# Blocks 0 and 1 of an attention and two-layer MLP kernel: the low part of a weight moves ahead on VectorE, PSUM banks turn otherwise, squares get four pairs of buffers, and a ring has four slots

## The chip, the cores and the metric

The kernel runs on one core of one Trainium2 chip. The metric is the device time of one launch in microseconds (us). Three runs of the kernel before took 1746.13, 1746.9 and 1747.65 us; the median is 1746.9 us.

## The reference

Keys and values are averaged over groups of eight positions, attention runs on those, and two matrix products with an activation between them follow, twice:

```python
scores = scale * np.matmul(q, k_p.transpose(0, 1, 3, 2))      # (8, 8, 576, 72)
attn = softmax(scores)
x = (attn @ v_p) as rows                                      # (4608, 512)
h = np.maximum(x @ w_in, 0.0);  x = h * h @ w_out             # first layer, 512 -> 2048 -> 512
h = x @ w_in2;                  out = np.maximum(0.01 * h, h) @ w_out2
```

## The kernel before, in words

The 4608 token rows are cut into nine blocks of 512. All numbers of a matrix product stand as a high and a low part, and a product is three matmuls: high by high, high by low, low by high. The hidden width of 2048 is cut into 16 chunks of 128.

Blocks 0 and 1 are done together, ahead of the others, because the weights arrive as 64-bit words while they run. `first_products` goes through 32 units, one for each pair of block and chunk, in the order of `ORDER`: chunks 0 to 11 of block 0, chunks 0 to 3 of block 1, chunks 12 to 15 of block 0, chunks 4 to 15 of block 1. A unit is 12 matmuls at L866 into one PSUM bank out of three (`acc_bank`, L863), a ReLU on ScalarE (L876) that empties the bank into a buffer `r`, and a store of `r` to the scratch tensor `mid` in DRAM, issued by GpSimd (L1056). From unit 20 on the buffers are a ring of eight slots, two tiles `xh` and `xl` (L1050). In units 1 to 11 the attention of block 1 runs beside the products (`second_attention`): maxima (L599), exponentials (L608), normalizing (L619 to L629), transposes on TensorE, their high copies on ScalarE (L660) and low parts on VectorE (L669), and the value products L701 to L704 with their split L678/L679.

The weights are converted meanwhile. One weight tile holds two chunks and passes through five steps, "a" to "e": a is ScalarE (L231); b is VectorE's L235 and L238; c is L249 and L252; d is VectorE's L293 and then ScalarE's copy L296, the high part; e is VectorE's L300, the low part, which reads what L296 wrote. `conversion(u)` starts tile n at the units of the table `begins`: every second unit for the first tiles (tile 5 begins at unit 8, tile 6 at 10, tile 7 at 12), and then at units 14, 16, 19, 21, 24, 26 and 29 for tiles 8 to 14. The beginning unit issues a of tile n+1 and c, d of tile n; the unit behind it issues b of tile n+1 and then e of tile n.

`second_products` then takes the 32 units again in order of block and chunk. It loads `r` from `mid` (L1066, on SP's queue), squares it on ScalarE (L879), splits the square into `gh` and `gl` on VectorE (L884, L885, two buffers each) and adds 12 matmuls (L905) to four accumulators, the banks 0 to 3. Beside it go the steps of block 2's attention, one now and then, and the conversion of the second layer's weights. The load runs six units ahead (`AHEAD`), the square three; in the last unit of `first_products` three squares are issued ahead of that unit's ReLU (L1041). Later blocks (`block`) and the second layer follow.

Every engine takes its instructions in the order in which the program issues them; no scheduler changes it.

Of the kernel before, what the change touches and what calls it, by code (L numbers as in the profile page):

```python
# [9 lines left out]
F32 = mybir.dt.float32  # L10
F32R = mybir.dt.float32r
# [5 lines left out]
P = 128  # L17
# [26 lines left out]
def attention_relu2_leaky_kernel(  # L44
# [21 lines left out]
    KC = DM // P  # L66
    FC = DFF // P
    RD = POOL * D
    RROWS = 6 * REM
    T = 512  # L70
# [27 lines left out]
    def sb(shape, dt, tag):  # L98
        pool = POOLS.get(tag, attn)
        return pool.tile(shape, dt, tag=tag, name=tag, bufs=BUFS.get(tag, 1))  # L100

    def bank():
        return psum.tile([P, 512], F32, tag="ps", name="ps", bufs=4)

    def acc_bank(m):
        return psum.tile([P, 512], F32, tag=f"acc{m}", name=f"acc{m}")

    def f32(ap):
        return ap.bitcast(F32)
# [209 lines left out]
    class Stored:  # L319
# [46 lines left out]
        def finish(self):  # L366
            while self.n < 12 * FC:
                self.tick()
# [312 lines left out]
    def x_tiles(dt=F32R):  # L681
        both = [sb([P, KC, T], dt, tag) for tag in ("xh", "xl")]
        return tuple([t[:, kc] for kc in range(KC)] for t in both)
# [166 lines left out]
    def value_steps(blk, t0):  # L850
        def piece(b):
            if b not in built:
                built.add(b)
                v_place(b)
            o, e = max(t0, b * S) - t0, min(t0 + T, (b + 1) * S) - t0
            values(blk, o, e - o)

        return [lambda b=b: piece(b) for b in batches_of(t0)]


    def first(blk, c, at=None):
        hi, lo = xsplit[blk]
        ps = bank() if at is None else acc_bank(at % (KC - 1))  # L863
        for kc in range(KC):
            for n, (w, x) in enumerate(((wih[c], hi), (wih[c], lo), (wil[c], hi))):
                nc.tensor.matmul(  # L866
                    ps,
                    lhsT=w[:, kc],
                    rhs=x[kc],
                    start=(kc == 0 and n == 0),  # L870
                    stop=(kc == KC - 1 and n == 2),
                )
        return ps

    def relu(r, ps):
        nc.scalar.activation(out=r, in_=ps, func=AF.Relu)  # L876

    def square(r):
        nc.scalar.activation(out=r, in_=r, func=AF.Square)  # L879

    def in_parts(r):
        gh = sb([P, T], F32R, "gh")
        gl = sb([P, T], F32R, "gl")
        nc.vector.tensor_copy(gh, r)  # L884
        nc.vector.tensor_tensor(out=gl, in0=r, in1=f32(gh), op=ALU.subtract)  # L885
        return gh, gl

    def between(blk, ps):
        r = sb([P, T], F32, "r")
        relu(r, ps)  # L890
        square(r)
        return in_parts(r)

    def second(c, acc, g):
        gh, gl = g
        wh, wl = woh[c], wol[c]
        ms = range(KC)
        passes = (wh, gh), (wl, gh), (wh, gl)
        if c < FC - 1:
            order = [(m, n) for m in ms for n in (0, 1)] + [(m, 2) for m in ms]  # L900
        else:
            order = [(m, n) for m in ms for n in (0, 1, 2)]
        for m, n in order:
            w, x = passes[n]
            nc.tensor.matmul(  # L905
                acc[m],
                lhsT=w[:, m * P : (m + 1) * P],
                rhs=x,
                start=(c == 0 and n == 0),
                stop=(c == FC - 1 and n == 2),  # L910
            )
# [14 lines left out]
    def block(blk, t0, steps, turn, chunk_done):  # L926
# [4 lines left out]
        def slot(i):  # L931
            nonlocal done
            upto = len(steps) if i >= N_SLOTS - 1 else len(steps) * (i + 1) // N_SLOTS
            while done < upto:
                steps[done]()
                done += 1

        g = between(blk, first(blk, 0))
        chunk_done("in", 0)
        for u in range(FC):  # L940
# [17 lines left out]
    w1, w2 = Weights(w1_in, w1_out), Stored(w2_in, w2_out)  # L958
# [13 lines left out]
    def second_attention():  # L972


        pe, behind, dve = ([[] for _ in range(FC)] for _ in range(3))
        blk, b = 1, 1
        pe[0] += [pooled_late[0], lambda: k_mask(b)]
        behind[0].append(lambda: k_transpose(b) or [])

        def both(u, fn):  # L980
            pe[u].append(lambda: dve[u].extend(fn()))

        for j, i in enumerate(range(T // P, 2 * T // P)):
            u = 1 + 2 * j
            pe[u].append(lambda i=i: (q_transpose(i), taken(("q", i))))
            both(u + 1, lambda i=i: score_products(i))
            dve[u + 2].append(lambda i=i: normalize(i))
            behind[u + 3].append(lambda i=i: [p_products(i, blk, T)])
        for n, (what, c) in enumerate([("v", c) for c in range(NP)] + [("rem", c) for c in range(2)]):
            both(3 + n, lambda what=what, c=c: [v_tile_pe(b, what, c)])  # L990
        turn = value_steps(blk, T)
        pe[6].append(turn[0])
        dve[9].append(lambda: v_split(b))

        def placed():
            built.add(b)
            v_place(b)

        pe[10].append(placed)
        pe[HEAD - 1].append(turn[1])  # L1000
        return pe, behind, dve

    def loads_of(u):

        if u < 2:
            load_q(6 + u)
        if u == 0:
            for c in range(NP):
                load_to(("v", 1, c), v_load(1, c), ("st", "st", "st", "gh")[c])
            for c in range(2):  # L1010
                load_to(("rem", 1, c), rem_load(1, c), "gl")
        if u == 0:
            w1.load(4)
        if u % 2 and u // 2 + 5 < FC - 1:
            w1.load(u // 2 + 5)
        if u == 2 * FC - 12:
            held.clear()
            load()


    begins = {2 * n - 2 if n < FC // 2 else FC - 2 + (n - FC // 2) * 5 // 2: n for n in range(1, FC - 1)}

    def conversion(u):
        if u in begins:
            n = begins[u]
            if n + 1 < FC - 1:
                w1.do("a", n + 1)
            w1.do("bcd" if n == 1 else "cd", n)
        elif u - 1 in begins:
            n = begins[u - 1]  # L1030
            if n + 1 < FC - 1:
                w1.do("b", n + 1)
            w1.do("e", n)

    def first_products():
        pe, behind, dve = second_attention()
        for u, (blk, c) in enumerate(ORDER):
            for fn in pe[u] if u < FC else ():
                fn()
            if u == 2 * FC - 1:  # L1040
                for n in range(3):  # L1041
                    square(mids[n])
                mids["parts"] = in_parts(mids.pop(0))
            ps = first(blk, c, u)
            rest = [x for fn in (behind[u] if u < FC else ()) for x in fn()]
            for fn in dve[u] if u < FC else ():
                fn()
            conversion(u)
            if u == FC + SIDE:
                ring.extend(x for t in x_tiles(F32) for x in t)  # L1050
            r = ring[c % len(ring)] if u >= FC + SIDE else sb([P, T], F32, "r")
            relu(r, ps)
            for fn in rest:
                fn()
            loads_of(u)
            nc.gpsimd.dma_start(out=mid[blk, c], in_=r)  # L1056
            if u >= 2 * FC - AHEAD:
                mid_load(u - 2 * FC + AHEAD)


    ring, mids, AHEAD = [], {}, 6

    def mid_load(u):
        if u < 2 * FC:
            r = mids[u] = ring[u % len(ring)]
            nc.sync.dma_start(out=r, in_=mid[u // FC, u % FC])  # L1066

    def second_products():
        steps, turn = all_steps[2], value_steps(2, 2 * T)
        n_units, done = 2 * FC, 0  # L1070
        w1.load(FC - 1)
        g = mids.pop("parts")
        for u in range(n_units):
            blk, c = divmod(u, FC)
            if c == 0:
                acc = [acc_bank(m) for m in range(KC)]
            mid_load(u + AHEAD)
            if u + 3 < n_units:
                square(mids[u + 3])
            if u + 1 < n_units:  # L1080
                g_next = in_parts(mids.pop(u + 1))
            if u >= n_units - 2:
                turn.pop(0)()
            second(c, acc, g)
            if 4 <= u < 9:
                w1.do("abcde"[u - 4], FC - 1)
            upto = len(steps) * u // (n_units - 3)
            while done < min(upto, len(steps)):
                steps[done]()
                done += 1  # L1090
            if u >= FC // 2:
                w2.tick()
            if c == FC - 1:
                finish(blk * T, acc)
            g = g_next
# [364 lines left out]
```

## Time and profile before

| What | Value |
|---|---|
| Median of three runs | 1746.9 us |
| The profiled execution's own time | 1745.2 us |
| Its span in the trace | 1743.3 us |
| TensorE (PE) busy | 1696.8 us, 97% of the span |
| VectorE (DVE) busy | 1110.9 us, 64% |
| ScalarE (ACT) busy | 627.8 us, 36% |
| First products of blocks 0 and 1 | 47 to 171.5 us |
| Second products of blocks 0 and 1 | 171.5 to 280 us |

The shares are means over the whole span. The change touches the first 280 us only, where TensorE is not always busy; times of the rows below are microseconds from the start of the span, the second number is a duration, and a bracket says how long the engine stood idle before the instruction and what ended that.

### The profile page before, as it was taken

To read this page: it belongs to the slowest core of one execution; us is meant where nothing else is said; L and a number is where in the kernel's file an instruction comes from. 1 tells how busy PE (TensorE), PEld (TensorE's weight loads), DVE (VectorE), ACT (ScalarE), POOL (GpSimd) and SP (SyncE) were. 2 spreads that over 40 slices of the span, in tenths; PEclk is the share of its full clock that TensorE was granted. 3 is DMA by queue.
4 is the path that set the end of the run, shared out by engine and by line. 5 is a ranking of instruction groups with operands and counts; after the bars stand their busy time and mean duration, and the time that the engine had idled before them with its cause. 6 is when DMAs were issued, how large, how long until landed. Compare 5 with 4: busy or idle time off the path is not lost.

```text
span 1743.3 us, 21699 instructions
## 1 busy us (share of the span) xinstructions
PE 1696.8 (97%) x8312; PEld 1462.6 (84%) x8312; DVE 1110.9 (64%) x2020; ACT 627.8 (36%) x1496; POOL 19.1 (1%) x39
## 2 busy tenths in 40 slices
PE   6889999999999999999999999999999999999999
PEld 5768778888888888888888899999899999999998
DVE  7888777666666666565434655665566675666564
ACT  4555244343443443433433322332332332233221
POOL 0012000000000000000000000000000000000000
PEclk9989999999999999999999999999999999999999
DMA  8914552323233332231004202202202411320320
GB/s 231 340 64 141 176 184 87 100 81 95 87 97 86 102 103 67 96 117 61 13 24 151 83 8 73 73 0 73 73 18 104 169 38 72 109 93 17 109 73 37
DMA packets 106296, 162.44 MB, mean 93 GB/s; under 512 B 44112, under 2 KB 44240, under 8 KB 105168
## 3 DMA queue, kind: packets, MB, share of 16 engines
q1 hardware_dynamic: 103632, 152.67, 26.4%
q0 software_dynamic: 2560, 8.39, 1.3%
q8 instruction: 65, 1.06, 0.3%
q14 instruction: 39, 0.32, 0.1%
HBM read 111.75 MB, written 49.28 MB: 92 GB/s over the span
## 4 chain that ended last, share of the span: by engine, by line
PE 90%; DVE 7%; ACT 2%; issue 1%; DMA 0%; SPq 0%; DVEq 0%; ACTq 0%
PE acc L905 20%; PE ps L1281 20%; PE ps L866 17%; PE acc L1348 15%; PE ps L1348 7%; PE acc L866 4%; PE ps L587 2%; PE ps L650 1%; PE ps L551 1%; ACT s L608 1%; PE ps L702 0%; PE ps L704 0%; PE ps L701 0%; PE ps L703 0%; DVE xl L679 0%
## 5 line engine op out<-in xcount | busy, mean ns | idle before, releaser
L905 PE MATMUL acc<-gh,wo 128*128 128x512 f32 x1152 | 297.6, 396 | 4.0 <-DVE gh L884 1.9
L866 PE MATMUL ps<-xh,wi 128*128 128x512 f32 x896 | 297.0, 394 | 0.0
L1281 PE MATMUL ps<-fh,wi 128*128 128x384 f32 x1344 | 289.1, 337 | 0.1
L1281 PEld LDWEIGHTS ps<-fh,wi 128*128 128x128 f32 x1344 | 243.1, 188 | 22.2 <-DVE gh L1294 0.4
L905 PEld LDWEIGHTS acc<-gh,wo 128*128 128x128 f32 x1152 | 213.9, 189 | 50.9 <-DVE gh L884 4.0
L1348 PE MATMUL acc<-wo,sh 128*128 128x512 f32 x768 | 205.6, 390 | 0.0
L866 PEld LDWEIGHTS ps<-xh,wi 128*128 128x128 f32 x896 | 168.2, 188 | 34.9 <-issue 0.2
L884 DVE CAST gh<-r 128x512 fp32r<-128x512 f32 x112 | 47.7, 426 | 199.4 <-ACT r L879 199.0
L866 PE MATMUL ps<-xl,wi 128*128 128x512 f32 x448 | 174.5, 390 | 0.0
L1281 PE MATMUL ps<-fl,wi 128*128 128x384 f32 x672 | 171.1, 336 | 0.0
L905 PE MATMUL acc<-gl,wo 128*128 128x512 f32 x576 | 159.7, 391 | 0.0
L1348 PEld LDWEIGHTS acc<-wo,sh 128*128 128x128 f32 x768 | 141.5, 188 | 15.6
L876 ACT ACTIVATE r<-ps 128x512 f32<-128x512 f32 x112 | 67.7, 604 | 212.0 <-PE ps L866 212.0
L905 PEld LDWEIGHTS acc<-gl,wo 128*128 128x128 f32 x576 | 108.8, 189 | 23.5
L1281 PEld LDWEIGHTS ps<-fl,wi 128*128 128x128 f32 x672 | 121.4, 188 | 0.0
L1348 PE MATMUL acc<-wo,sl 128*128 128x512 f32 x384 | 120.3, 392 | 0.0
L608 ACT ACTIVATE s<-ps,m 128x72 f32<-128x72 f32 x240 | 72.3, 331 | 102.0 <-DVE m L599 102.0
L1348 PE MATMUL ps<-wo,sh 128*128 128x512 f32 x384 | 102.8, 389 | 0.0
L1294 DVE TENSOR_TENSOR u<-gh,ps 128x384 f32<-128x384 f32 x48 | 26.6, 554 | 119.0 <-PE ps L1281 119.0
L866 PEld LDWEIGHTS ps<-xl,wi 128*128 128x128 f32 x448 | 84.2, 188 | 16.6
L1348 PEld LDWEIGHTS acc<-wo,sl 128*128 128x128 f32 x384 | 72.1, 188 | 18.3 <-DVE sl L1329 3.7
L885 DVE TENSOR_TENSOR gl<-r,gh 128x512 fp32r<-128x512 f32 x112 | 77.6, 693 | 7.7 <-PE acc L905 0.5
(206 smaller groups left out, 2366.4 us busy)
## 6 DMA issues: line engine op xcount, KB each, us to landing
wi<-in_moe_w_in SPq DMA_DIRECT2D x8, 1024.0 KB
wo<-in_moe_w_out SPq DMA_DIRECT2D x8, 1024.0 KB
val<-in_moe_w_in SPq DMA_DIRECT2D x16, 512.0 KB
val<-in_moe_w_out SPq DMA_DIRECT2D x16, 512.0 KB
w2p<-val SPq DMA_DIRECT2D x16, 512.0 KB
wo<-w2p SPq DMA_DIRECT2D x8, 1024.0 KB
xh<-x SPq DMA_DIRECT2D x10, 768.0 KB
xl<-x SPq DMA_DIRECT2D x10, 768.0 KB
```

The costliest lines, as they stand in the source:

```text
L551: nc.tensor.transpose(ps[:, cc * P : (cc + 1) * P], raw[:, cc * P : (cc + 1) * P], ident)
L587: nc.tensor.matmul(ps[: r0 + n, c2 * PAIR : (c2 + 1) * PAIR], lhsT=qt[:, cc, : r0 + n], rhs=kts[b][:, keys], start=True, stop=True,)
L608: nc.scalar.activation(out=s[:, g, :], in_=ps[:, h * SP : (h + 1) * SP], func=AF.Exp, bias=m[:, g : g + 1], accum_out=None if i in early e ...
L650: nc.tensor.transpose(ps[:, cc * P : (cc + 1) * P], flat[:, cc * PAIR : cc * PAIR + P], ident)
L866: nc.tensor.matmul(ps, lhsT=w[:, kc], rhs=x[kc], start=(kc == 0 and n == 0), stop=(kc == KC - 1 and n == 2),)
L876: nc.scalar.activation(out=r, in_=ps, func=AF.Relu)
L884: nc.vector.tensor_copy(gh, r)
L885: nc.vector.tensor_tensor(out=gl, in0=r, in1=f32(gh), op=ALU.subtract)
L905: nc.tensor.matmul(acc[m], lhsT=w[:, m * P : (m + 1) * P], rhs=x, start=(c == 0 and n == 0), stop=(c == FC - 1 and n == 2),)
L1281: nc.tensor.matmul(at, lhsT=w[:, FORMS[j], kc], rhs=x[j][:, kc], start=m == 0 and j in (0, 1, 4), stop=m == 5, skip_group_check=True,)
L1294: nc.vector.tensor_tensor(out=out_, in0=x, in1=at, op=ALU.add)
L1348: nc.tensor.matmul(self.acc[i], lhsT=x[g % 2][c][t][:, at], rhs=self.outs[p][:, part_, c], start=p == 0 and m == 0, stop=p == PAIRS - 1 an ...
```

## The change

Five things move, all in blocks 0 and 1.

- Step e of a tile leaves `conversion` and is issued earlier in its unit: ahead of the attention's VectorE work of that unit (`dve[u]`) and ahead of step b of the next tile.
- `first` takes bank (u + 2) mod 3 in place of u mod 3.
- The ring has four slots, the tile `xh`; the tile `xl` becomes two further pairs of buffers for the squares' parts (`more`), taken in turn with the old ones.
- `AHEAD` is 4 in place of 6, the square runs two units ahead in place of three, and two squares in place of three stand ahead of the last ReLU.
- In units 15 and 31 of `second_products` no step of block 2's attention is issued.

```diff
     def first(blk, c, at=None):
         hi, lo = xsplit[blk]
-        ps = bank() if at is None else acc_bank(at % (KC - 1))
+        ps = bank() if at is None else acc_bank((at + 2) % (KC - 1))
...
-    def in_parts(r):
-        gh = sb([P, T], F32R, "gh")
-        gl = sb([P, T], F32R, "gl")
+    def in_parts(r, to=None):
+        gh, gl = to or [sb([P, T], F32R, tag) for tag in ("gh", "gl")]
...
                 w1.do("b", n + 1)
-            w1.do("e", n)
...
             if u == 2 * FC - 1:
-                for n in range(3):
+                for n in range(2):
                     square(mids[n])
                 mids["parts"] = in_parts(mids.pop(0))
             ps = first(blk, c, u)
             rest = [x for fn in (behind[u] if u < FC else ()) for x in fn()]
+            if u - 1 in begins:
+                w1.do("e", begins[u - 1])
             for fn in dve[u] if u < FC else ():
                 fn()
             conversion(u)
             if u == FC + SIDE:
-                ring.extend(x for t in x_tiles(F32) for x in t)
+                one, two = sb([P, KC, T], F32, "xh"), sb([P, KC, T], F32R, "xl")
+                ring.extend(one[:, n] for n in range(KC))
+                more.extend((two[:, n], two[:, n + 1]) for n in (0, 2))
...
-    ring, mids, AHEAD = [], {}, 6
+    ring, more, mids, AHEAD = [], [], {}, 4
...
-            if u + 3 < n_units:
-                square(mids[u + 3])
+            if u + 2 < n_units:
+                square(mids[u + 2])
             if u + 1 < n_units:
-                g_next = in_parts(mids.pop(u + 1))
+                g_next = in_parts(mids.pop(u + 1), more[(u + 1) % 2] if (u + 1) % 4 > 1 and u + 3 < n_units else None)
...
-            while done < min(upto, len(steps)):
+            while c < FC - 1 and done < min(upto, len(steps)):
```

On VectorE in unit 9 of the first products, between the low parts of a transposed tile (L669) and the normalizing of the next (L619), the rows stand like this; `wi_907` is the tile whose low part unit 10 multiplies by:

```order
 L669 TENSOR_TENSOR ptl<-ps,pth 128x4x128
 L669 TENSOR_TENSOR ptr<-ps,ptr 32x2x128
+L300 TENSOR_TENSOR wi_907<-val,wi_907 128x1024
 L619 TENSOR_REDUCE l<-s 128x8
 L620 TENSOR_SCALAR l<-l 128x8
```

Before, that L300 stood behind the whole normalizing, the split of the values and L235, L238 of the next tile; now it stands ahead of them. Units 3, 5 and 7 show the same move.

On VectorE from unit 12 on, where only weights are left, each tile has this piece (`wo_1101` is one tile, `wo_947` the words of the next):

```order
 L293 TENSOR_TENSOR val<-val,wo_852 128x1024
+L300 TENSOR_TENSOR wo_1101<-val,wo_1101 128x1024
 L235 TENSOR_SCALAR val<-wo_947 128x1024
 L238 SCALAR_TENSOR_TENSOR val<-wo_947,val 128x1024
-L300 TENSOR_TENSOR wo_1101<-val,wo_1101 128x1024
 L249 TENSOR_SCALAR wo_947<-val 128x1024
 L252 SCALAR_TENSOR_TENSOR wo_947<-wo_947 128x1024
 L293 TENSOR_TENSOR val<-val,wo_947 128x1024
```

L235 and L238 stood between L293 and the L300 that waits for ScalarE's copy of its result; now L300 follows L293 at once.

On ScalarE at the end of the first products, before (the three L876 are the ReLUs of units 29, 30 and 31):

```order
L296 CAST wo_1408<-val 128x1024
L876 ACTIVATE xl<-acc_1392 128x512
L876 ACTIVATE xl<-acc_1413 128x512
L879 ACTIVATE xh<-xh 128x512 x3
L876 ACTIVATE xl<-acc_1437 128x512
```

And now, in the same place:

```order
L296 CAST wo_1406<-val 128x1024
L876 ACTIVATE xh<-acc_1390 128x512
L876 ACTIVATE xh<-acc_1411 128x512
L879 ACTIVATE xh<-xh 128x512 x2
L876 ACTIVATE xh<-acc_1434 128x512
```

The second of the two squares reads ring slot 1, which now holds unit 29's result until that is stored and chunk 1 of block 0 is loaded into it; before, chunks 0 to 2 were loaded in units 26 to 28, into slots that units 24 to 26 had used.

## Rows read from the trace of the kernel before

**Rows 1.** The page's busy line: busy us (share) xinstructions of each engine.
```profile
PE 1696.8 (97%) x8312; PEld 1462.6 (84%) x8312; DVE 1110.9 (64%) x2020; ACT 627.8 (36%) x1496; POOL 19.1 (1%) x39
```

**Rows 2.** Two stretches: us, busy of PE, PEld, DVE, ACT, POOL, granted clock, DMA.
```profile
100.00:110.00 10.00, 5.80 (x16) 4.42 (x16) 7.06 (x10) 2.15 (x7) 0.69 (x2) 0.50 0.15 54
130.00:140.00 10.00, 10.00 (x46) 8.28 (x45) 9.83 (x10) 4.80 (x7) 2.71 (x5) 1.00 0.35 130
```

**Rows 3.** Timeline of PE, first products: start, us, instruction, idle before and its releaser.
```profile
46.82 0.47 PE L866 MATMUL acc<-xh,wi 128*128 128x512 f32 x1 [2.09 <-DVE qt L391]
...
54.90 1.39 PE L587 MATMUL acc<-kt,qt 128*128 128x144 f32 x8 [1.08 <-ACT qt L556]
...
98.75 0.50 PE L866 MATMUL acc<-xh,wi 128*128 128x512 f32 x1 [1.60 <-ACT wi L296]
...
104.20 1.22 PE L866 MATMUL acc<-xh,wi 128*128 128x512 f32 x2 [4.71 <-DVE wi L300]
```

**Rows 4.** Timeline of DVE in units 5 to 10.
```profile
72.43 0.75 DVE L619 TENSOR_REDUCE l<-s 128x8 f32<-128x576 f32 x1 [0.55 <-ACT s L608]
...
85.39 0.75 DVE L619 TENSOR_REDUCE l<-s 128x8 f32<-128x576 f32 x1 [0.28 <-ACT s L608]
...
96.80 0.75 DVE L619 TENSOR_REDUCE l<-s 128x8 f32<-128x576 f32 x1 [0.55 <-ACT s L608]
...
101.07 0.68 DVE L235 TENSOR_SCALAR val<-wi 128x1024 uint32<-128x1024 uint32 x1
...
110.34 0.69 DVE L669 TENSOR_TENSOR ptl<-ps,pth 128x512 fp32r<-128x512 f32 x1 [3.07 <-ACT pth L660]
```

**Rows 5.** Timeline of ACT in units 5 and 7.
```profile
73.28 1.07 ACT L296 CAST wi<-val 128x1024 fp32r<-128x1024 f32 x1
...
86.23 1.08 ACT L296 CAST wi<-val 128x1024 fp32r<-128x1024 f32 x1
```

**Rows 6.** Timeline of DVE, weights alone: one round, and the last tile.
```profile
126.79 1.23 DVE L293 TENSOR_TENSOR val<-val,wo 128x1024 f32<-128x1024 f32 x1
127.93 0.69 DVE L235 TENSOR_SCALAR val<-wo 128x1024 uint32<-128x1024 uint32 x1
128.65 1.23 DVE L238 SCALAR_TENSOR_TENSOR val<-wo,val 128x1024 uint32<-128x1024 uint32 x1
129.79 1.22 DVE L300 TENSOR_TENSOR wo<-val,wo 128x1024 fp32r<-128x1024 f32 x1
...
131.66 1.23 DVE L252 SCALAR_TENSOR_TENSOR wo<-wo 128x1024 f32<-128x1024 uint32 x1
132.93 1.23 DVE L293 TENSOR_TENSOR val<-val,wo 128x1024 f32<-128x1024 f32 x1
...
163.59 1.23 DVE L293 TENSOR_TENSOR val<-val,wo 128x1024 f32<-128x1024 f32 x1
165.93 1.23 DVE L300 TENSOR_TENSOR wo<-val,wo 128x1024 fp32r<-128x1024 f32 x1 [1.11 <-ACT wo L296]
```

**Rows 7.** Timeline of ACT at the end of the first products.
```profile
164.85 1.05 ACT L296 CAST wo<-val 128x1024 fp32r<-128x1024 f32 x1 [0.69 <-DVE val L293]
...
169.50 1.66 ACT L879 ACTIVATE xh<-xh 128x512 f32<-128x512 f32 x3
171.72 0.60 ACT L876 ACTIVATE xl<-acc 128x512 f32<-128x512 f32 x1 [0.56 <-ACT xh L879]
```

**Rows 8.** Stores of L1056 from issue to landing.
```profile
DMA to landing us min/median/max: 2.3/2.6/8.5
```

**Rows 9.** Timeline of SP: the load of `mid` for unit 7.
```profile
181.28 0.32 SPq L1066 DMA_DIRECT2D xl<-mid  x1
```

**Rows 10.** Timeline of ACT: the square that waited for that load.
```profile
184.11 0.63 ACT L879 ACTIVATE xl<-xl 128x512 f32<-128x512 f32 x1 [1.85 <-DMA xl<-mid]
```

**Rows 11.** Timeline of PE: the start of the second products.
```profile
172.37 1.67 PE L905 MATMUL acc<-gh,wo 128*128 128x512 f32 x6 [0.28 <-ACT xl L876]
```

**Rows 12.** The page's groups: L905, busy, mean ns, idle before and its largest releaser.
```profile
L905 PE MATMUL acc<-gh,wo 128*128 128x512 f32 x1152 | 297.6, 396 | 4.0 <-DVE gh L884 1.9
```

## The prediction, made before the run

> **What bounds the kernel now.** I read the busy line first: TensorE works 97% of the span [rows 1]. What can be won lies in the few microseconds in which it stands idle; a loss can come from any place where the change makes another engine late. So I went to the stretch that the change touches, 47 to 280 us, and asked for TensorE's idle times there. Up to unit 10 of the first products it waits for VectorE and ScalarE; the largest waits are 1.60 us for the high part of tile 5 and 4.71 us for its low part, L300 [rows 3]. Behind these two waits the granted clock is 0.50, the lower of the two levels (1.2 against 2.4 GHz), and 16 instructions took 5.80 us [rows 2]: half of that, 2.9 us, is what the clock cost. From unit 12 on TensorE never stops, but VectorE has almost nothing to spare: 9.83 of 10 us busy [rows 2], with one weight tile every 6.14 us (L293 to L293, 126.79 to 132.93) [rows 6]. The last of its tiles makes the rule visible: where no other work stands between L293 and L300, L300 waits 1.11 us for ScalarE's copy L296 [rows 6].
>
> That is what decides. The edit puts every L300 right behind what it must wait for, on an engine that is full, and takes away the work that covered the wait.
>
> **Units 0 to 11.** The bank turn first. Unit 0 waited 2.09 us for a bank that VectorE still had to read (L391) [rows 3]; another bank takes that away. But 8 us later TensorE waits 1.08 us for ScalarE's copy of a transposed tile [rows 3], which hangs on VectorE's queue and doesn't move, so that wait becomes longer instead: 0, with 2.1 us as the most it could give.
>
> Now step e. L296 comes behind the eight exponentials and L231 on ScalarE, and normalizing L619 needs the exponentials alone. So L300 ahead of L619 holds VectorE up until L296 is done, and gives back 1.14 us (129.79 less 128.65) [rows 6] where it stood before.
>
> - Unit 5: L296 ends at 74.35 [rows 5], L300 takes 1.14, L619 starts at 75.5 in place of 72.43 [rows 4]. VectorE is 3.1 late, and 1.9 once L300's old place is past.
> - Unit 7: what feeds L296 is late by this 1.9, so it ends at 87.31 + 1.9 = 89.2 [rows 5]; L619 at 90.35 in place of 85.39 [rows 4]; 3.8 late in the end.
> - Unit 9: VectorE had come to L619 0.55 early, at 96.25 [rows 4]; it now comes there at 100.05, when L296 is just done. L300 ends at 101.2, so TensorE has tile 5's low part 2.9 us sooner than at 104.20 [rows 3]. L619 starts at 101.2, 4.4 late.
>
> The gain doesn't last. L235 moves from 101.07 to 105.5. From it to L669 VectorE had 6.2 us of work (110.34 less the 3.07 idle, less 101.07) [rows 4], now 1.14 less and 0.13 more for an instruction that reads the one ahead of it (131.66 to 132.93 takes 1.27, not 1.14) [rows 6]. So L669 starts at 110.7, where it started at 110.34 [rows 4]. The value products wait for it: 0.3 us later than before, although unit 10 was earlier.
>
> TensorE then stands idle from about 104.5 (101.3, ten matmuls and six transposes) to 111.3, but for a few matmuls. The nearest row is the pair of waits of 1.60 and 4.71 us with the clock at 0.50 behind them [rows 2, 3]. If the value products fall into such a stretch, 14 of them at 0.2 us more each make 2.8; if not, 0. I take 2.0. The first part: 0.3 + 2.0 = 2.3 us later (bounds -2 and 3.1; the lower one, if TensorE's earlier unit 10 brings the transposes and all behind them forward).
>
> In the Trainium skill (TensorE: Matmul & The Clock Gate, "HAM oscillation — how this bites in real kernels") waits for data make the array's clock fall to half, and the work after each is done at that rate. The trace agrees at 104.20, the one long wait it has in this stretch. By that rule this place and the next such one below would count in full, 2.8 and 2.9 in place of 2.0 and 2.4, and the sum would be 16.5 us in place of 15.2.
>
> **Units 12 to 31.** From the value splits on, VectorE has weights alone. A round was 6.14. Now L293 to L300 takes 2.34 (163.59 to 165.93) in place of 1.14, and L238 is followed by an instruction that reads its result, 1.27 in place of 1.14 [rows 6]: 1.33 more, 7.47 us. PE's 12 matmuls take about 2.72 us a unit, and tiles 8 to 14 begin 2.5 units apart, 6.8 us. So VectorE is now slower than TensorE asks for. The low parts are not what is missed (they are used in the second products); the ReLUs are. ScalarE issues L296 ahead of its unit's ReLU, and TensorE needs that ReLU three units on to have the bank. Seven rounds lie between tiles 7 and 14, so the last L296 ends at 165.90 [rows 7] + 0.13 + 7 x 1.33 = 175.3, plus the first part.
>
> TensorE itself loses less: unit 29's bank hangs on L296 one round earlier, 8.1 late. It ended at 158.7 + 1.05 (one round of 6.14 ahead of 164.85) [rows 7], its ReLU at 160.3, and unit 29 began at 163.3 (unit 31 ended at 171.5 [rows 11], less three units); with 3.0 to spare TensorE is 5.1 late.
>
> **The turn to the second products.** Unit 29's ReLU follows the last L296 and ends at 175.9 (0.60) [rows 7]. Its buffer is slot 1. It is stored (2.3 at least) [rows 8], at 178.2; chunk 1 of block 0 is loaded there (issue 181.28 to the square at 184.11, 2.8) [rows 9, 10], at 181.05; squared (0.55, a third of 1.66) [rows 7]; and only behind this square stands the ReLU of unit 31 (0.60) [rows 7], which ends at 182.2. Unit 31 now has bank 0, and the second products begin with accumulator 0. Before, they began at 171.5 and waited 0.28 [rows 11], as if at 171.75. That is 10.45 us later, plus the first part. TensorE's own lateness of 5.1 lies inside.
>
> It is idle for some 5.5 us there (176.6 to 182.2, with the first part in both). By the 4.71 us wait, the clock falls, and 2.9 us go; if it doesn't, 0. I take 2.4.
>
> **Second products.** The four pairs let VectorE split squares ahead of TensorE. All its waits for gh are 1.9 us in total [rows 12], and they arise where VectorE is full with pooling and weights, so I take 0 (bounds -1.9 and, for loads that come late with four units of lead, +4). The guard on units 15 and 31 does nothing: 27 steps are spread as 27 u / 29, which is 13 for unit 14 and for unit 15, and all are done by unit 29.
>
> **Sum.** 2.3 + 10.45 + 2.4 = 15.2 us later. The profiled execution took 1745.2 us, 1.7 under the median; 1745.2 + 15.2 = 1760.4, and from the median of 1746.9, 1762.
>
> **Rivals.**
>
> 1. Faster: L300's wait is covered. Then the 4.71 us and the 2.9 us of slow clock go and nothing takes their place: 1746.9 - 7.6 = 1739. It decides if VectorE has more than 1.33 us a round to spare. For it: VectorE is busy 64% over all [rows 1], and the 3.07 us idle at 110.34 [rows 4]. Against it: 9.83 of 10 [rows 2]. Chance 0.05.
> 2. The turn is hidden: the square of chunk 1 doesn't hold the last ReLU (loads faster, or VectorE catches up). TensorE's own 5.1 and the first part's 2.3 stay, less the 0.28: 1754. Against it: store and load together took 5.1 us in the rows, two units. Chance 0.15.
> 3. The ring of four also starves the second products. SP's queue is in order, and a load behind a blocked one has two units less of lead; squares then hold ScalarE. With the +4 above, 1766. For it: a square already waited 1.85 us for a load [rows 10]. Chance 0.12.
> 4. The waits cancel, and the time stays as it was: the 7.6 us won at unit 10 pay for the late turn. It needs the value products 5 us or more ahead, which L669's place at 110.7 denies. Chance 0.03.
>
> My forecast has 0.65: 1762, by itself 1757 to 1766. A difference under 0.2%, 3.5 us, is what this kernel's measurement can't tell from none. Slower by more than that: the forecast, rivals 2 and 3, 0.92; within: 0.04, rival 4 and a piece of 1; faster 0.04. The range of 1755 to 1767 holds the forecast with both ends of the clock's cost (4.4 below, 1.3 above), most of rival 3 and the upper part of rival 2.
>
> **What would show it.** In the profile after: L300 idle some 1.1 us before each of tiles 7 to 13, L293 to L293 at 7.5 us; L866 waits for ReLUs (L876) or ScalarE between units 17 and 29; L879 waiting for a load from mid ahead of the last L876, and L905's first matmul waiting some 5 us for it; the granted clock at 0.50 there. Unit 10's low part sooner by about 3 us, and L669 no sooner. I am wrong if L293 to L293 stays near 6.1 us, if unit 31's ReLU doesn't stand behind a load, or if the value products come earlier than 111.

## The result, and the profile after

The changed kernel took 1763.45 us (median of 5 runs, 1761.06 to 1765.97); the kernel before, beside it, 1746.9 us (5 runs, 1746.08 to 1748.71). The ratio is 1.0096, 95% interval 1.0084 to 1.0107: 16.5 us slower by the medians. The forecast was 1762. The profiled span is 1761.7 us, 18.4 more than before. Of that, 17.6 stand at unit 1 of the second products, and the lateness stays at 17.5 to 17.7 up to 560 us. Another 0.5 comes about 600 us. A low stretch of the clock at 711 us, 3.4 us longer than the one before at 694, adds 1.6, and the same is gained back at 803 us, where only the execution before had a low stretch.

The busy line (columns as in [rows 1]) shows that no engine has much more to do. TensorE's 7 us more are for the most part work done at the low clock: 28.6 us of its work fell into low stretches in this trace, 16.2 in the one before, and half of the 12.5 us between them is 6.2. The rest of the loss is idle time.

```profile
PE 1703.8 (97%) x8312; PEld 1466.8 (83%) x8312; DVE 1112.7 (63%) x2020; ACT 628.1 (36%) x1496; POOL 19.2 (1%) x39
```

TensorE's waits from 40 to 290 us in the kernel after (engine, line waited for: us in total, times, longest us):

```profile
PE acc L904 <- ACT xh L876: 5.7, 1, 5.7
PE ps L703 <- DVE ptl L669: 4.0, 1, 4.0
PE acc L587 <- ACT qt L556: 3.4, 2, 3.2
PE ps L381 <- DVE ptl L669: 2.6, 2, 1.9
PE acc L866 <- ACT xh L876: 2.3, 2, 1.1
PE acc L866 <- ACT r L876: 2.1, 2, 1.8
...
PE ps L701 <- DVE st L679: 1.4, 1, 1.4
...
PE acc L904 <- DVE gh L883: 1.1, 3, 0.5
...
PE acc L904 <- DVE xl L883: 0.6, 2, 0.4
...
PE acc L866 <- DVE wi L300: 0.5, 1, 0.5
```

The wait for L300, 4.71 us before [rows 3], is down to 0.5. In its place stand 3.2 us at L587 (two waits of 2.09 and 1.08 before), 1.4 at L701 in unit 6, 4.0 for L669 a few microseconds behind unit 10's L300, 4.4 us for ReLUs (L876) within the first products, and 5.7 us for the last ReLU at the turn. The same waits in the timeline of TensorE (start, us, instruction, idle before and its releaser), to be held against [rows 3] and [rows 11]:

```profile
54.56 1.39 PE L587 MATMUL acc<-kt,qt 128*128 128x144 f32 x8 [3.16 <-ACT qt L556]
...
81.41 0.30 PE L701 MATMUL ps<-pth,v_hi 128*128 128x64 f32 x1 [1.36 <-DVE st L679]
...
102.81 0.50 PE L866 MATMUL acc<-xh,wi 128*128 128x512 f32 x1 [1.66 <-ACT wi L296]
104.07 1.22 PE L866 MATMUL acc<-xh,wi 128*128 128x512 f32 x2 [0.53 <-DVE wi L300]
...
114.07 0.74 PE L703 MATMUL ps<-ptl,v_hi 128*128 128x448 f32 x1 [3.96 <-DVE ptl L669]
...
142.88 0.50 PE L866 MATMUL acc<-xh,wi 128*128 128x512 f32 x1 [1.75 <-ACT r L876]
...
187.16 3.78 PE L904 MATMUL acc<-gh,wo 128*128 128x512 f32 x8 [5.72 <-ACT xh L876]
```

VectorE in the attention's units and behind them, the answer to [rows 4] and [rows 6]. L300 now waits for L296: 1.64 and 2.73 us in units 5 and 7, and 1.1 us in every round of the weights; in unit 9 (102.79) and for the tile behind it the copy is there in time. The last two L293 shown stand 7.53 us apart, where it was 6.14, and so do all the rounds that follow, within 0.01.

```profile
75.47 1.22 DVE L300 TENSOR_TENSOR wi<-val,wi 128x1024 fp32r<-128x1024 f32 x1 [1.64 <-ACT wi L296]
...
91.88 1.23 DVE L300 TENSOR_TENSOR wi<-val,wi 128x1024 fp32r<-128x1024 f32 x1 [2.73 <-ACT wi L296]
...
102.79 1.23 DVE L300 TENSOR_TENSOR wi<-val,wi 128x1024 fp32r<-128x1024 f32 x1
103.93 0.75 DVE L619 TENSOR_REDUCE l<-s 128x8 f32<-128x576 f32 x1
...
113.33 0.69 DVE L669 TENSOR_TENSOR ptl<-ps,pth 128x512 fp32r<-128x512 f32 x1
...
132.50 1.23 DVE L293 TENSOR_TENSOR val<-val,wo 128x1024 f32<-128x1024 f32 x1
134.84 1.23 DVE L300 TENSOR_TENSOR wo<-val,wo 128x1024 fp32r<-128x1024 f32 x1 [1.12 <-ACT wo L296]
...
140.03 1.22 DVE L293 TENSOR_TENSOR val<-val,wo 128x1024 f32<-128x1024 f32 x1
```

ScalarE at the turn, the answer to [rows 7] and [rows 10]: behind the last L296 come the ReLUs of units 29 and 30, then the two squares, the second 3.19 us idle for its load, and only then the ReLU of unit 31.

```profile
178.92 1.05 ACT L296 CAST wo<-val 128x1024 fp32r<-128x1024 f32 x1 [5.00 <-DVE val L293]
179.88 1.07 ACT L876 ACTIVATE xh<-acc 128x512 f32<-128x512 f32 x2
182.17 0.63 ACT L879 ACTIVATE xh<-xh 128x512 f32<-128x512 f32 x1 [1.22 <-DMA xh<-mid]
185.99 0.63 ACT L879 ACTIVATE xh<-xh 128x512 f32<-128x512 f32 x1 [3.19 <-DMA xh<-mid]
186.53 0.58 ACT L876 ACTIVATE xh<-acc 128x512 f32<-128x512 f32 x1
```

The chain of waits of the kernel after goes through just this place, store, load, square and ReLU (start us, us, what):

```profile
180.87 2.31 DMA mid<-xh
183.31 2.65 DMA xh<-mid
185.99 0.04 ACT xh L879
...
186.53 0.59 ACT xh L876
...
187.16 10.95 PE acc L904 x36
```

And two stretches of the kernel after (us, busy of PE, PEld, DVE, ACT, POOL, granted clock, DMA share, GB/s). From 130 on VectorE, 9.83 us busy before [rows 2], is busy 8.67: it is slower, and idle, because it waits. Behind the 5.7 us wait the granted clock is 0.50, the lower of the two levels.

```profile
130.00:140.00 10.00, 9.69 (x43) 7.68 (x42) 8.67 (x9) 3.10 (x4) 1.12 (x2) 1.00 0.21 79
187.00:192.00 5.00, 4.84 (x11) 3.80 (x12) 1.89 (x4) 0.74 (x2) 0.54 (x1) 0.50 0.34 100
```

How late the units end, after less before, in the two profiled executions: 4.2 us at unit 11, 9.8 at unit 31; the second products begin 15.7 late, and at their unit 1 it is 17.6. One caution belongs to all such differences of single executions: the end of unit 0 alone lay between 0.1 us sooner and 2.6 us later than before in kernels that are alike up to there. Sums are therefore made of medians below, and traces are used for what happens inside a stretch.

### The profile page after: what moved, and what is told of

The parts are those of the page before. It is cut to its first block, busy times and chain, and to the rows that moved or that the text cites. A ratio compares the mean times of both kernels' runs of the same rounds, so it can differ in the third digit from the quotient of the medians.

```text
span 1761.7 us, 21689 instructions
## 1 busy us (share of the span) xinstructions
PE 1703.8 (97%) x8312; PEld 1466.8 (83%) x8312; DVE 1112.7 (63%) x2020; ACT 628.1 (36%) x1496; POOL 19.2 (1%) x39
## 4 chain that ended last, share of the span: by engine, by line
PE 85%; DVE 6%; issue 5%; ACT 2%; POOL 1%; DMA 1%; SPq 0%; POOLq 0%; DVEq 0%; ACTq 0%
PE acc L904 20%; PE ps L1283 20%; PE ps L866 17%; PE acc L1350 15%; PE ps L1350 7%; PE ps L587 2%; PE ps L650 1%; POOL mid L1058 1%; PE ps L551 1%; ACT s L608 1%; DVE xl L679 0%; PE ps L702 0%; DVE qt L418 0%; PE ps L701 0%; ACT r L876 0%
## 5 line engine op out<-in xcount | busy, mean ns | idle before, releaser
L904 PE MATMUL acc<-gh,wo 128*128 128x512 f32 x1040 | 269.3, 397 | 9.1 <-ACT xh L876 5.7
L904 PEld LDWEIGHTS acc<-gh,wo 128*128 128x128 f32 x1040 | 194.4, 190 | 51.7 <-ACT xh L876 6.1
L904 PE MATMUL acc<-gl,wo 128*128 128x512 f32 x520 | 144.7, 393 | 0.0
L876 ACT ACTIVATE r<-ps 128x512 f32<-128x512 f32 x112 | 67.7, 604 | 212.2 <-PE ps L866 208.1
L904 PEld LDWEIGHTS acc<-gl,wo 128*128 128x128 f32 x520 | 98.6, 190 | 21.2
```

What stands on the lines that cost most here:

```text
L904: nc.tensor.matmul(acc[m], lhsT=w[:, m * P : (m + 1) * P], rhs=x, start=(c == 0 and n == 0), stop=(c == FC - 1 and n == 2),)
```

## The experiments

Two theories stood after the result. **A**, the prediction's: three separate losses (VectorE held up in the attention's units; the longer weight round; the ring of four at the turn), each by its own instructions. **B**: one of them alone makes the loss (the ring, say) and the others only show waits that TensorE would have anyway. Each diff says which kernel it changes; `HEAD` in them is 12, the first unit with weights alone. A ratio is to the kernel before, run on the same chip.

### One part at a time

**All but step e** (the kernel after, step e back behind b):

```diff
                 w1.do("b", n + 1)
+            w1.do("e", n)
...
-            if u - 1 in begins:
-                w1.do("e", begins[u - 1])
```

> The change without its first part: step e stands where it stood before, the bank turn, the ring of four, the four pairs and the guard stay. My theory: units 0 to 31 run as before, and only the turn is later: the last L296 ends at 165.9, unit 29's ReLU at 166.9, its store lands at 169.2, the load of chunk 1 at 172.0, the square ends at 172.5 and unit 31's ReLU at 173.1, so the second products begin 1.4 us late: 1748.3 us (1747.5 to 1750). Rival A, the ring itself is most of the loss: 8 us or more over before, 1755 or more. Rival B, the four pairs gain in the second products: faster than before.

Measured: 1752.58 us, ratio 1.0032 (1.0019 to 1.0044), 5.6 us over its before. The expectation was too low. Its trace is 4.0 us late at the end of unit 2, behind the wait that the bank turn makes (see there), and 3.7 at unit 31. At the turn the second square waits for its load, though the last L296 is late by those 3.7 us and no more (timeline of ScalarE):

```profile
176.38 0.63 ACT L879 ACTIVATE xh<-xh 128x512 f32<-128x512 f32 x1 [1.12 <-DMA xh<-mid]
176.92 0.58 ACT L876 ACTIVATE xh<-acc 128x512 f32<-128x512 f32 x1
```

TensorE waited 2.2 us for that ReLU and ran at the low clock for 3.4 us behind it. So the ring costs something without step e, which my working had tied to the late L296.

**Step e alone** (the kernel before, with the three marked lines above changed the other way):

> The kernel before with step e early and nothing else. My theory: L293 to L293 is 7.5 us, unit 31 ends 9.8 us late as in the changed kernel; the ring of eight has chunks 0 to 2 loaded long ago, so behind unit 30's ReLU (ends near 181.3) stand three squares (1.66) and unit 31's ReLU: accumulator 1 is free near 183.6, 11.4 us late: 1758.3 us (1756 to 1761). Rival A, an early step e costs only through the ring: about 4 us from units 0 to 11, 1751. Rival B, the early step is harmless and the ring does it all: within 1 us of before. With the run without step e this tells whether the two parts add up: 1.4 and 11.4 are 12.8, and 17.5 was measured; what is missing, 4 to 5, is the ring meeting a late ReLU.

Measured: 1758.18 us, ratio 1.0064 (1.0051 to 1.0078), 11.2 us slower, as expected. 11.2 and 5.6 make 16.8, against 16.5 for the whole change: the two parts add, and I had reckoned with several microseconds that arise only from both together. B falls here: step e carries two thirds, and the rest costs something without it.

**Step e early in the attention's units only** (the kernel before; from unit 12 on as it was):

```diff
-            w1.do("e", n)
+            if u >= HEAD:
+                w1.do("e", n)
...
+            if u < HEAD and u - 1 in begins:
+                w1.do("e", begins[u - 1])
```

> The kernel before with step e early in units 0 to 11 alone, beside the attention; from unit 12 on it stands as before. My theory: the first part of the loss alone, unit 10 sooner by 2 to 3 us, the value products later by 2 to 4 us, and nothing added after unit 12: 1750 us (1748.5 to 1751.5). Rival, the early low part pays where TensorE waits for it (4.71 us at unit 10): 1743 to 1746.

Measured: 1750.73 us, ratio 1.0025 (1.0015 to 1.0035), 4.1 us slower, as expected. From unit 12 on its TensorE never waited until the turn. Step e's 11.2 us are therefore 4.1 in the attention's units and, by the difference of the medians, 7.1 in the weights' rounds. Its waits between 108 and 172 us are these two; the gain at unit 10 is given back some microseconds later:

```profile
PE ps L703 <- DVE ptl L669: 4.0, 1, 4.0
PE ps L701 <- ACT pth L660: 2.1, 1, 2.1
```

**The bank turn alone** (the kernel before):

```diff
-        ps = bank() if at is None else acc_bank(at % (KC - 1))
+        ps = bank() if at is None else acc_bank((at + 2) % (KC - 1))
```

> The kernel before with the bank turn (u + 2) mod 3 alone. My theory after the first runs: unit 0 begins 2.1 us sooner, but the wait for ScalarE's copy at unit 2 takes it up and becomes one wait of 3.2 us in place of 2.1 and 1.1, and the granted clock falls to 0.50 behind it for 3.4 to 6.8 us, as in every trace so far that has this bank turn: 1.7 to 2.8 us lost there and 0.5 at the second products, where unit 31 now has bank 0: 1749.3 us (1748.2 to 1750.5). Rival, the prediction's term: 0 at units 0 to 2 and at most 0.5 at the turn, 1747.3, the clock at 1.00 between 50 and 70 us.

Measured: 1746.98 us (11 runs) beside 1746.59, ratio 1.0003 (0.9995 to 1.0012): no change. The wait that it removes at unit 0 came back as the longer one at L587, 3.18 us where 1.08 stood [rows 3], and the clock fell behind it (timeline of TensorE, and a window with the columns as above, its clock 0.66):

```profile
56.09 1.56 PE L587 MATMUL acc<-kt,qt 128*128 128x144 f32 x8 [3.18 <-ACT qt L556]
```

```profile
56.00:61.00 5.00, 4.91 (x19) 3.58 (x20) 2.35 (x4) 1.90 (x8) 1.09 (x2) 0.66 0.82 245
```

I had taken that fall for a loss, and the expectation built on it failed. In this one trace the loss is there: units 2 to 31 end 2.4 to 2.7 us late. The low stretch at unit 10 was 6.8 us in place of 10.2, but it gave nothing back (unit 9 ends 2.5 late, unit 11 2.4). Over 11 executions the median did not move all the same. One possible reason, not shown for the kernel before: of the seven traces here without the bank turn, three (step e alone, step e in the attention's units, and the version with two repairs) have a low stretch of 3.4 us at 48 us, behind the wait of 2.09 us, and these are the three whose unit 0 ends 2.6 late; the other four have none. So the clock at units 0 to 2 differs from execution to execution, and a fall read from one trace is not yet a price.

**The ring of four without step e and the bank turn** (the first experiment, its bank turn taken back; the shorter leads, the four pairs and the guard are still in):

> The run without step e, now without the bank turn too: the ring of four, the loads four and the squares two units ahead, the four pairs and the guard. That run was 5.6 us slower, of which its trace places 3.5 at the turn to the second products and the rest in units 0 to 11, where the bank turn alone cost 0.4 in the median of its runs. My theory: the turn alone remains, 3 to 3.5 us: 1750 us (1749 to 1751.5). Rival A, the parts meet: without the bank turn the second products start with a bank that is free, the ReLU of unit 31 is needed 0.5 us later, and under 1.5 us remain, 1748. Rival B, all 5.6 remain, 1752, and the ring costs something beyond the turn.

Measured: 1749.4 us (11 runs) beside 1746.51, ratio 1.0013 (1.0004 to 1.0022), 2.9 us slower, as expected. In its trace units up to 31 are 0.7 late, and unit 1 of the second products 4.0: 3.3 us at the turn. On ScalarE:

```profile
173.81 0.63 ACT L879 ACTIVATE xh<-xh 128x512 f32<-128x512 f32 x1 [1.82 <-DMA xh<-mid]
174.34 0.58 ACT L876 ACTIVATE xh<-acc 128x512 f32<-128x512 f32 x1
```

The wait at the turn is 1.7 us, and the clock is low for 3.4 us behind it. 2.9 and 0.4 make 3.3 of the 5.6; the other 2.3 us of bank turn and ring together stay open (the interval of the 5.6 is 3.3 to 7.7). The trace of the two together has a low stretch of 6.8 us at 55 us, but after what the bank turn alone taught I do not call that shown.

### Where the late conversions reach TensorE

**The square of chunk 1 behind the last ReLU** (the kernel after):

```diff
-                for n in range(2):
-                    square(mids[n])
+                square(mids[0])
...
             relu(r, ps)
+            if u == 2 * FC - 1:
+                square(mids[1])
```

> The changed kernel with the square of chunk 1 issued behind unit 31's ReLU instead of ahead of it. My theory: the ReLU no longer waits for the load; it ends near 182.4 and the second products begin near 182.5 in place of 187.2. Their second unit then waits for the square (load at 186.0, parts ready at 186.9), so 4 to 5 us of the 17 are won: 1759 us (1757 to 1761). Rival, the load is needed at once anyway and TensorE only waits one unit later, with the same loss of clock: under 1.5 us won, 1762 or more.

Measured: 1760.31 us, ratio 1.0079 (1.0065 to 1.0093): 3.1 us won, inside the expected range, though less than the 4 to 5 of its theory. The wait of 5.72 us became two, for the ReLU and then for the split of the square that is now late, and the clock stayed at its upper level:

```profile
186.13 2.08 PE L904 MATMUL acc<-gh,wo 128*128 128x512 f32 x8 [1.45 <-ACT xh L876]
...
190.74 2.11 PE L904 MATMUL acc<-gh,wo 128*128 128x512 f32 x8 [1.60 <-DVE gh L883]
```

The turn costs 3.8 us here where it cost 7.7. So the 5.7 us did hang on the square that waits for a store and a load.

**The ReLU ahead of the conversion, from unit 12 on** (the kernel after):

```diff
-            conversion(u)
+            if u < HEAD:
+                conversion(u)
...
             relu(r, ps)
+            if u >= HEAD:
+                conversion(u)
```

> The changed kernel with each unit's ReLU issued ahead of its conversion steps from unit 12 on, so that it doesn't stand behind L296 of its own unit; VectorE's order is unchanged. My theory: L293 to L293 stays at 7.5 us, but TensorE's waits for ReLUs between units 17 and 29 shrink from 5.6 us to under 3 (the next unit's ReLU still stands behind L296), and unit 29's ReLU is on time, so that the turn waits less: 4 to 5 us won, 1759 us (1756 to 1761). Rival, TensorE is held by the rate of VectorE and not by where the ReLU stands on ScalarE: no change, 1763.

Measured: 1757.34 us, ratio 1.0065 (1.005 to 1.008): 6.1 us won, inside the expected range and more than the 4 to 5 of its theory. VectorE's round is as long as ever (timeline of VectorE, 7.53 us from L293 to L293):

```profile
133.46 1.23 DVE L293 TENSOR_TENSOR val<-val,wo 128x1024 f32<-128x1024 f32 x1
...
140.99 1.22 DVE L293 TENSOR_TENSOR val<-val,wo 128x1024 f32<-128x1024 f32 x1
```

Yet from unit 12 to 31 TensorE loses 2.9 us in place of 5.6, and the wait at the turn is 3.3 us in place of 5.7. What is left between units 12 and 31 are again two waits for ReLUs, 2.3 us, none for L296 or L300. The late tiles hurt through ReLUs that stand behind L296 in ScalarE's queue, as the prediction had it; they are not themselves waited for.

### Can the gain at unit 10 be kept?

**L300's wait covered by step b** (the kernel before, b and then e both ahead of the attention's work):

```diff
-        elif u - 1 in begins:
-            n = begins[u - 1]
-            if n + 1 < FC - 1:
-                w1.do("b", n + 1)
-            w1.do("e", n)
...
+            if u - 1 in begins:
+                n = begins[u - 1]
+                if n + 1 < FC - 1:
+                    w1.do("b", n + 1)
+                w1.do("e", n)
```

> The kernel before with steps b and e of conversion, in their old order, both ahead of the attention's VectorE work of the unit. My theory: b (1.87 us) covers ScalarE's L231 and L296 (1.95 us), so that L300 finds its input ready and VectorE doesn't stand idle; tile 5's low part comes 4 us sooner, the weights' rounds stay at 6.14 us, and the value products begin 2 to 3 us sooner: 1745 us (1743.5 to 1747). If the clock falls again, the same as before. Rival, whatever is put ahead of normalizing makes the attention late by its own length: 3 us slower, 1750.

Measured: 1750.92 us, ratio 1.0025 (1.0015 to 1.0035), 4.3 us slower: the expectation of a gain failed. L300 no longer waited at unit 9, but b and e, 3 us together, now stand ahead of the attention's own work in every second unit. After unit 5's, TensorE waits 1.75 us for L391, the clock falls, and the last matmul of unit 6 starts 4.6 us late (timeline, then a window):

```profile
79.06 0.30 PE L701 MATMUL ps<-pth,v_hi 128*128 128x64 f32 x1 [1.75 <-DVE vp L391]
```

```profile
80.00:88.00 8.00, 7.89 (x30) 6.51 (x30) 4.86 (x10) 0.81 (x4) 0.00 (x0) 0.57 1.05 386
```

**That, with two repairs**: L669 of the last transposed tile ahead of c and d in unit 10, and the ReLU first from unit 12 on.

```diff
+            if u == HEAD - 2:
+                while rest:
+                    rest.pop(0)()
-            conversion(u)
+            if u < HEAD:
+                conversion(u)
...
+            if u >= HEAD:
+                conversion(u)
```

> As the run in which b covers e, and two edits more: in unit 10 the low part of the last transposed tile (L669) goes ahead of steps c and d of tile 6, and from unit 12 on each ReLU is issued ahead of its unit's conversion. My theory: the value products no longer stand behind 4 us of weight work and come 4 to 6 us sooner than before; VectorE then reaches its weights no sooner, but the ReLUs don't wait for them: 1742.5 us (1740 to 1745). Rival, VectorE's rate holds TensorE whatever the order: within 1 us of the run in which b covers e.

Measured: 1746.72 us beside 1746.59, ratio 1.0001 (0.9992 to 1.0010): no change; the expectation of 1742.5 failed. The repairs win the 4 us back, no more. TensorE falls back by 4.9 us in unit 6 as in the experiment before.

**Steps b and e early in unit 9 only**, with the same two repairs (the kernel before; the repairs' lines are those above and not repeated):

```diff
-        elif u - 1 in begins:
+        elif u - 1 in begins and u != 9:
...
+            if u == 9:
+                w1.do("b", 6)
+                w1.do("e", 5)
```

> The kernel before with steps b and e ahead of the attention's VectorE work in unit 9 alone, the low part L669 ahead of steps c and d in unit 10, and ReLUs ahead of conversion from unit 12 on. My theory: units 0 to 8 as before; tile 5's low part comes 4 us sooner; the value products don't stand behind weight work and come 3.5 us or more sooner; the rest moves with them: 1743.3 us (1741 to 1745.5). Rival, as in the run with all units: a longer single wait makes the clock fall and nothing is left, 1746 to 1748.

Measured: 1744.7 us (11 runs, 1741.64 to 1748.0) beside 1746.51, ratio 0.9991 (0.9982 to 1.0000): 1.8 us faster, inside the expected range, the fastest version here, but with an interval that reaches 1.0000, so hardly told from the kernel before. In its trace all of the gain, 3.0 us, arises at unit 10. The repairs were not run without the early steps, so a share of theirs in the 1.8 is not excluded. TensorE's long wait is 1.46 us in place of 4.71, and nothing takes its place:

```profile
101.19 1.22 PE L866 MATMUL acc<-xh,wi 128*128 128x512 f32 x2 [1.46 <-DVE wi L300]
...
107.36 0.47 PE L701 MATMUL ps<-pth,v_hi 128*128 128x448 f32 x1 [0.32 <-ACT pth L660]
```

## Why the prediction was right

Forecast 15.2 us slower, measured 16.5 by the medians; 1762 against 1763.45. Step by step, with its own names:

| Step | Predicted | Measured |
|---|---|---|
| L300 at unit 5, start | 74.35 | 75.47 |
| L300 at unit 7, start | 89.2 | 91.88 |
| L669 at unit 10 | 110.7 | 113.33 |
| Tile 5's low part at TensorE | 2.9 sooner than 104.20 | 104.07, 0.1 sooner |
| Value products that need L669, start | 0.3 later | 3.0 later |
| Clock on the value products | 2.0 | 1.3 |
| First part (units 0 to 11) | 2.3 (-2 to 3.1) | 4.2 in the profile, 4.1 (2.6 to 6.1) for step e alone |
| Wait of L300 per weight round | 1.11 | 1.11 and 1.12 |
| Round, L293 to L293 | 7.47 | 7.53 |
| TensorE's own lateness, units 12 to 31 | 5.1 | 5.6 |
| Store and load at the turn | 2.3 + 2.8 | 2.31 + 2.65 |
| Wait at the turn | 5.5 | 5.72 |
| Clock behind the turn | 2.4 | 2.6 by itself, 2.0 as a difference to before |
| Bank turn | 0 | 0.4 (-0.9 to 2.1), not told from 0 |

**The weight rounds and the turn** came out as worked. The round came from one row of the kernel before, the last tile, where nothing covered L300's wait [rows 6]; every round after looks like it. The row that speaks for the chain is the ReLU of unit 31 behind two squares; the run that shows it is the experiment with the square behind. The clock: the second products began 15.7 us late, their unit 1 was 17.6 late, 2.0 more. Their unit 0 took 5.29 us at the lower level, and unit 1 of the kernel before 2.72 at the upper one, so the clock by itself cost 2.6; the difference is smaller because unit 0 took 3.34 us before as well, the wait of 0.28 [rows 11] among them. By the Trainium skill (TensorE: Matmul & The Clock Gate, "HAM oscillation — how this bites in real kernels") both places would have counted in full, 2.8 at the value products and 2.9 here. The trace agrees on both falls (0.50 from 113.9 for 3.4 us, and from 187 to 192) and has their prices at 1.3 and 2.6.

**The first part was mis-sized**, the one term outside its bounds in the profile, and in two directions. The value products that need L669 start 2.98 us later and not 0.3; the stretch from there to unit 11, for 3.3 us of it at the lower clock, takes 1.27 longer, where I had 2.0. These are the first of them and the first matmul of unit 11, before and then after (timeline of TensorE; the first one after, at 114.07, stands above):

```profile
111.09 0.47 PE L703 MATMUL ps<-ptl,v_hi 128*128 128x448 f32 x1
...
114.31 0.39 PE L866 MATMUL acc<-xh,wi 128*128 128x512 f32 x1
```

```profile
118.56 0.39 PE L866 MATMUL acc<-xh,wi 128*128 128x512 f32 x1
```

From L619 on the working holds: L669 follows L619 of unit 9 by 9.40 us (103.93 to 113.33), predicted 9.5. What failed is the start, "what feeds L296 is late by this 1.9": L296 of unit 7 started 4.5 us late (90.76 against 86.23 [rows 5]), so L300 of unit 7 started 2.7 us later than I had it, and everything down to L669 kept these 2.7. That is also why the sign "unit 10's low part sooner by about 3 us" did not come: it was 0.1 sooner.

```profile
87.39 0.59 ACT L660 CAST pth<-ps 128x512 fp32r<-128x512 f32 x1 [4.65 <-PE ps L650]
...
90.76 1.09 ACT L296 CAST wi<-val 128x1024 fp32r<-128x1024 f32 x1
```

ScalarE stood 4.65 us idle for TensorE's transposes ahead of the exponentials and L296. I had taken TensorE as on time in these units and let VectorE's lateness reach it at the value products alone. In the changed kernel it has new waits ahead of them, 3.16 us at L587 and 1.36 at L701, where VectorE's split L679 now comes late, and behind each the clock was low for 3.4 us, at 55.9 and 83.2; unit 5 ends 2.0 late, unit 6 4.6. With step e early in the attention's units and no bank turn (4.1 us by the medians) it goes by another place: a wait of 2.30 us for L669 ahead of unit 5, where 0.99 stood before, and the clock low for 3.4 us from 75.7; unit 4 ends 1.6 late, unit 5 4.6. There the 10.2 us at the lower level that began at 99.9 before begin at 109.8, about the wait for L669.

**What was right by a wrong path.** I had the ring's loss follow from the late last L296. The ring without step e loses 2.9 us with L296 in time: in its trace the store takes 2.57 us, the load is issued only behind it and takes 3.06, and its square still stands ahead of the last ReLU. Since step e alone takes 11.2 and the rest 5.6, the total came out, but the attribution in my first two expectations did not: they put the two at 11.4 and 1.4 and left the rest to their meeting. The steps read from the two traces sum to 17.6 us; the medians give 16.5, because the execution traced before was 1.7 us under its median. Within the first part an error of 2.7 us met one of 0.7 the other way, which is luck.

**The rivals.** Rival 1 (faster, 1739) asked for more than 1.33 us a round to spare on VectorE; it had 0.17 of 10, and the round grew by 1.39. Rival 2 (turn hidden, 1754) is denied by the 5.72 us. Rival 3 (starving second products, 1766) lies near in the time but not in the trace: past unit 1 the lateness stays at 17.5 to 17.7 us, and the waits for the squares' high parts there are 1.1 us for `gh` and 0.6 for the pairs in `xl`, where `gh` had 1.9 before. So the trace shows neither a loss nor a gain from the four pairs and the guard, as taken; neither was run alone. Rival 4 (the waits cancel) is denied by the 16.5 us.

## What to carry to other kernels

An instruction moved ahead in an in-order queue brings its wait with it: ask what used to stand in that gap, and if the engine is full there, count the exposed wait once per round, then look for who stands behind the late result on the next engine (here ReLUs behind copies that nobody needed yet). A smaller ring puts a store and a load, 5 us here, ahead of whatever is queued behind their consumer. And move an instruction only in the one unit where its lateness is waited for: with the same two repairs, steps b and e early in every second unit changed nothing (1746.72 us), and in unit 9 alone they gave 1.8 (1744.7), as far as that can be told from none.

## What was not expected of the hardware

In all five traces with the bank turn, one wait of 3.2 us in place of two (2.09 and 1.08) was followed by 3.4 or 6.8 us at the lower clock. Of the seven traces with the two waits, three had 3.4 us at the lower clock behind the first and four had none. In those three unit 0 ended 2.6 us later than in the execution shown before, and the second wait then was 0.2 us in place of 1.08, so that unit 2 was only 1.7 late. Kernels that are alike up to unit 0 ended it up to 2.7 us apart, which is more than most single steps here are worth. And how long a wait is does not tell alone whether a fall follows: behind 1.36 us at 81.41 the clock fell, behind 1.75 at 142.88 in the same trace it did not.
